# Sigmoid attention and a gated feed-forward on one core: weight decoding in two tiles over all stages, operands made ahead, token differences on VectorE

## Chip, core, metric

The kernel runs on one NeuronCore of a Trainium2 chip. The metric is the device time of one execution in microseconds (us), the median of several runs. TensorE (PE) multiplies, VectorE (DVE), ScalarE (ACT) and GpSimd (POOL) do elementwise work, and SyncE (SP) issues nearly all DMAs, in order.

## What is computed

```python
scores = scale * np.matmul(q, k.transpose(0, 1, 3, 2)) - np.log(S)   # q, k, v: (8, 12, 448, 64)
attn = 1.0 / (1.0 + np.exp(-scores))
attn_out = np.matmul(attn, v)
x = np.ascontiguousarray(attn_out.transpose(0, 2, 1, 3)).reshape(B * S, H * D)   # (3584, 768)
h = x @ w_in                                   # (768, 2048)
g = h * np.clip(h + 3.0, 0.0, 6.0) / 6.0
return (g @ w_out).astype(np.float32)          # (2048, 768)
```

The weights come as 64-bit floats and are turned into 32-bit floats on the chip.

## The kernel before

**Pairs and products.** Both matrix products use a scheme with 7 block products in place of 8: `P1, P5, P6, P2, P7, P3, P4`, in this order. Tokens are taken as pairs of batches, `n` = 0 to 3; the four blocks of `x` are the two batches (of 448 tokens) by the two halves of the features. Each of the seven left operands is a block or a sum of differences of blocks. Full precision comes from splitting each operand in a high and a low part (fp32r) and adding three passes; so an operand for product `k` and feature chunk `c` (0 to 2) is a tile `X[n, k, c]` with two halves, made by `put`: a cast (L216) and a subtraction (L217), both on DVE. `minus` (L221) makes the differences, on POOL. `t_ops` sets out seven puts and four differences for each chunk. The tiles of `X` have one buffer each, so pair `n` can fill one only when pair `n - 1` has used it for its last product.

**Stages.** TensorE's order is attention of batches 0 to 3, the first feed-forward product of pair 0, attention of batch 4, product of pair 1, batches 5 and 6, product of pair 2, batch 7, product of pair 3, and then the second product of all pairs. A batch has 21 steps: for each, `scores` fills two PSUM banks (L169, L174), `sigmoid` on ACT (L180) reads them, and `av` (L194, L200) multiplies by v, two steps behind. When the 128 columns of two heads are complete, `take` copies one bank (ACT, L208) and adds the other (DVE, L209) into `xr[b, hp]`; only then may the two banks be filled again, three steps later.

**Quads.** The product of a pair is eight `quad`s, of 7 x 9 matmuls each (L279). Several products share a bank: P6, P7 and P4 are added to the bank of P1. So `seed2` (DVE, L295), which reads that bank after P6, has to be done before P7 starts, and `h22` (DVE, L299), which reads it after P7, before P4. The gates (ACT L313, DVE L316), differences of gates (L320 to L326) and the splitting of weights for the next quad (`split_w1`: ACT L252, DVE L253) fill ACT and DVE beside. The last gate of a stage reads the bank of P1, which attention's scores then use again.

**Weight decoding.** `prep(which, j, place, gap)` decodes block `j` of eight of the first (`which` = 0) or second weight matrix, in two halves `u`. `load` fetches raw 64-bit words to `st` (two buffers), `head` (ACT, L100) and `body` (five operations on DVE, L106 to L112, and an addition on POOL, L115) make 32-bit floats of a half in the tile `wt`, `sums` (POOL, L122, four operations) makes the weight sums of the scheme, and `store` writes all seven to DRAM, from where the quads load them again (L246). `wt` has a single buffer.

**Order.** Every piece is given a place in planned us with `at(place, f, *args)`. The list is sorted by place, and on PE, ACT, DVE and POOL the instructions run in that order, each engine in order by itself; a late instruction holds those behind it. SP's order is chosen by the framework's scheduler. Planned time `TU` = 1.863 us stands for one block product.

```python
    for j in range(HF):
        prep(0, j, 12 + 15.2 * j, 6)
    for j, place in enumerate([marks[0] + 10 + 30 * i for i in range(3)] + [marks[1] + 10 + 30 * i for i in range(3)] + [starts[2] + 5, starts[2] + 25]):
        prep(1, j, place, 8)
```

`starts[n]` is the planned start of a stretch of attention, `marks[n]` its end, where the quads of pair `n` start. So the first matrix is decoded beside batches 0 to 3, the second beside the quads of pairs 0 and 1 (three blocks each) and batches 5 and 6 (two).

Of the kernel before, what the change touches and what calls it, by code (L numbers as in the profile page):

```python
# [43 lines left out]
def tile_kernel(ctx: ExitStack, tc: tile.TileContext, qk, vP, w8, outT):  # L44
# [37 lines left out]
    def prep(which, j, place, gap):  # L82

        src = w8[which]
        st, wt = {}, {}
        slots = ((P1, P2), (P4, NW))

        def two(u):
            a, b = slots[u]
            return wt[0][:, a : b + 1 : b - a]  # L90

        def load(u):
            st[u] = att.tile([P, 2, W, 2], I32, tag="st", name=f"st_{which}_{j}_{u}", bufs=2)
            s = src[j, :, 2 * u * W : 2 * (u + 1) * W].rearrange("p (h n) t -> p h n t", h=2)
            nc.sync.dma_start(out=st[u], in_=s)

        def head(u):
            if u == 0:
# [1 line left out]
            nc.scalar.activation(two(u), st[u][:, :, :, 1].bitcast(F32), AF.Abs, bias=0.0, scale=2.0**-112)  # L100

        def body(u):
            low, high = st[u][:, :, :, 0], st[u][:, :, :, 1]
            a, e = two(u), high.bitcast(F32)
            ai = a.bitcast(I32)
            nc.vector.tensor_scalar_min(a, a, F64_TOP)  # L106
            nc.vector.tensor_scalar(out=ai, in0=ai, scalar1=3, scalar2=None, op0=ALU.logical_shift_left)
            nc.vector.scalar_tensor_tensor(
                out=ai, in0=high, scalar=-(2**31), in1=ai, op0=ALU.bitwise_and, op1=ALU.bitwise_or
            )  # L110
            nc.vector.tensor_scalar(out=high, in0=ai, scalar1=-(2**23), scalar2=None, op0=ALU.bitwise_and)
            nc.vector.scalar_tensor_tensor(  # L112
                out=e, in0=low.bitcast(U32), scalar=2.0**-52, in1=e, op0=ALU.mult, op1=ALU.mult
            )
            nc.gpsimd.tensor_tensor(out=a, in0=a, in1=e, op=ALU.add)  # L115

        def sums():
            w = wt[0]
            for o, x, y, op in (
                (P5, NW, P4, ALU.add), (P6, P5, P1, ALU.subtract), (P7, P1, NW, ALU.subtract), (P3, P2, P6, ALU.subtract)  # L120
            ):
                nc.gpsimd.tensor_tensor(out=w[:, o], in0=w[:, x], in1=w[:, y], op=op)  # L122

        def store():
            w = wt[0]
            if which == 0:
                nc.sync.dma_start(out=wd1[j], in_=w[:, :NW])
# [90 lines left out]
        X[n, k, c] = x  # L218

    def minus(o, x, y):  # L220
        nc.gpsimd.tensor_tensor(out=xr[o], in0=xr[x], in1=xr[y], op=ALU.subtract)  # L221
# [235 lines left out]
    for n, bs in enumerate(runs):
        steps = [(b, m, r) for b in bs for m in range(HC) for r in range(LC)]  # L460
# [90 lines left out]
```

## Time and profile before

| | us |
|---|---|
| median of 3 runs (lowest, highest) | 1287.93 (1285.09, 1294.91) |
| the profiled execution | 1288.0 |
| its span, first to last instruction | 1286.2 |
| PE busy | 1143.3 (89%) |
| DVE busy | 839.1 (65%) |
| ACT busy | 613.5 (48%) |
| POOL busy | 203.5 (16%) |
| mean granted TensorE clock | 0.942 |

The profile shows one execution. In its rows, `L174 PE MATMUL sc<-qk` is line 174 of the kernel, the engine, the operation and what it writes and reads; in a timeline, the first number is the start in the span, the second the duration, and the brackets give how long the engine sat idle before it, and what ended that. A row of the waits is "engine line <- what it waited for: us in total, times, longest". A row of the stretches gives for each engine the busy time and, in brackets, the number of instructions, and at its end the granted clock (1.00 is full speed), the share of the DMA engines and GB/s. `za` is the bank shared by P1, P6, P7 and P4, `zb` the others.

### The profile page before, as it was taken

To read this page: it belongs to the slowest core of one execution; us is meant where nothing else is said; L and a number is where in the kernel's file an instruction comes from. 1 tells how busy PE (TensorE), PEld (TensorE's weight loads), DVE (VectorE), ACT (ScalarE), POOL (GpSimd) and SP (SyncE) were. 2 spreads that over 40 slices of the span, in tenths; PEclk is the share of its full clock that TensorE was granted. 3 is DMA by queue.
4 is the path that set the end of the run, shared out by engine and by line. 5 is a ranking of instruction groups with operands and counts; after the bars stand their busy time and mean duration, and the time that the engine had idled before them with its cause. 6 is when DMAs were issued, how large, how long until landed. Compare 5 with 4: busy or idle time off the path is not lost.

```text
span 1286.2 us, 17828 instructions
## 1 busy us (share of the span) xinstructions
PE 1143.3 (89%) x6720; PEld 884.8 (69%) x6720; DVE 839.1 (65%) x1096; ACT 613.5 (48%) x830; POOL 203.5 (16%) x150
## 2 busy tenths in 40 slices
PE   8676777888799886978999987999999999999998
PEld 3222223777747776633899557989999999999997
DVE  3388534877798877596667594776565565565563
ACT  5443455433265433655444643445445544545542
POOL 2245343312240322053000130000000000000000
PEclk9777788988899988989999988999999999999999
DMA  6744456767646876554677339757645344345341
GB/s 241 264 165 158 175 191 211 273 242 258 228 131 190 269 261 223 186 170 144 209 236 229 132 116 336 217 189 282 247 158 186 144 157 158 117 166 204 115 137 64
DMA packets 90661, 250.20 MB, mean 195 GB/s; under 512 B 10064, under 2 KB 62672, under 8 KB 85072
## 3 DMA queue, kind: packets, MB, share of 16 engines
q1 hardware_dynamic: 90432, 249.01, 56.4%
q8 instruction: 52, 0.85, 0.3%
q14 instruction: 33, 0.27, 0.1%
q10 hardware_dynamic: 144, 0.07, 0.0%
HBM read 164.63 MB, written 84.41 MB: 194 GB/s over the span
## 4 chain that ended last, share of the span: by engine, by line
PE 48%; DVE 5%; DMA 2%; issue 1%; POOL 1%; ACT 1%; ACTq 0%; DVEq 0%; POOLq 0%
PE y L404 21%; PE yb L404 11%; PE za L279 8%; PE zb L279 6%; DVE x L217 2%; DMA raw<-wd 1%; DVE x L216 1%; PE sc L174 1%; PE pv L200 1%; DVE w L253 1%; DVE xr L209 0%; POOL wt L122 0%; DMA wd<-wt 0%; POOL xr L221 0%; ACT w L252 0%
## 5 line engine op out<-in xcount | busy, mean ns | idle before, releaser
L279 PE MATMUL za<-x,w 128*128 128x448 f32 x1152 | 273.4, 388 | 60.1 <-DVE zb L295 47.6
L404 PE MATMUL y<-x,w 128*128 128x448 f32 x1344 | 308.8, 365 | 0.0
L279 PEld LDWEIGHTS za<-x,w 128*128 128x128 f32 x1152 | 227.0, 200 | 94.1 <-DVE zb L295 53.2
L404 PEld LDWEIGHTS y<-x,w 128*128 128x128 f32 x1344 | 252.4, 188 | 20.0
L253 DVE TENSOR_TENSOR w<-w,w 128x768 fp32r<-128x768 f32 x112 | 107.3, 958 | 152.2 <-ACT w L252 150.8
L180 ACT ACTIVATE a<-sc,bias_s 128x896 f32<-128x896 f32 x168 | 168.2, 1009 | 77.4 <-PE sc L174 58.7
L174 PE MATMUL sc<-qk 64*64 64x448 f32 x1152 | 164.0, 589 | 44.7 <-ACT a L180 39.6
L279 PE MATMUL zb<-x,w 128*128 128x448 f32 x864 | 196.3, 372 | 2.7 <-DVE x L216 1.7
L252 ACT CAST w<-w 128x768 fp32r<-128x768 f32 x112 | 93.6, 836 | 191.4 <-PE yb L404 183.8
L253 DVE TENSOR_TENSOR w<-raw,w 128x768 fp32r<-128x768 f32 (+1 forms) x128 | 125.6, 982 | 90.0 <-ACT w L252 82.5
L279 PEld LDWEIGHTS zb<-x,w 128*128 128x128 f32 x864 | 166.8, 193 | 17.9 <-DVE x L216 2.1
L404 PE MATMUL yb<-x,w 128*128 128x448 f32 x672 | 172.6, 365 | 0.0
L200 PE MATMUL pv<-a,v 64*64 64x448 f32 x1152 | 165.6, 580 | 6.9 <-DVE xr L209 6.9
L174 PEld LDWEIGHTS sc<-qk 64*64 64x64 f32 x1152 | 51.9, 144 | 121.6 <-issue 59.3
L404 PEld LDWEIGHTS yb<-x,w 128*128 128x128 f32 x672 | 126.2, 188 | 10.0
L387 DVE TENSOR_TENSOR x<-gr,x 128x896 fp32r<-128x896 f32 x112 | 121.4, 1084 | 5.6 <-ACT x L386 5.6
L115 POOL TENSOR_TENSOR wt<-wt,st 128x768 f32<-128x768 f32 x32 | 62.5, 1954 | 366.8 <-DVE st L112 347.3
L200 PEld LDWEIGHTS pv<-a,v 64*64 64x64 f32 x1152 | 55.3, 144 | 81.8 <-issue 67.4
L386 ACT CAST x<-gr 128x896 fp32r<-128x896 f32 x112 | 105.3, 940 | 5.6 <-DMA gr<-gd 5.6
L252 ACT CAST w<-raw 128x768 fp32r<-128x768 f32 (+1 forms) x128 | 95.5, 748 | 13.5 <-DMA raw<-wd 13.5
L221 POOL TENSOR_TENSOR xr<-xr,xr 128x448 f32<-128x448 f32 x48 | 63.1, 1319 | 188.7 <-DVE x L217 186.5
L217 DVE TENSOR_TENSOR x<-xr,x 128x448 fp32r<-128x448 f32 x84 | 87.3, 1039 | 2.9
(48 smaller groups left out, 794.6 us busy)
## 6 DMA issues: line engine op xcount, KB each, us to landing
gr<-gd SPq DMA_DIRECT2D x28, 1792.0 KB, 8.0
raw<-wd SPq DMA_DIRECT2D x96, 384.0 KB, 3.6
gd<-ga SPq DMA_DIRECT2D x96, 224.0 KB, 3.5
qk<-qk SPq DMA_DIRECT2D x47, 448.0 KB, 5.1
gd<-gc SPq DMA_DIRECT2D x64, 224.0 KB, 2.8
st<-wi SPq DMA_DIRECT2D x16, 768.0 KB, 4.3
st<-wo SPq DMA_DIRECT2D x16, 768.0 KB, 5.8
v<-vP SPq DMA_DIRECT2D x48, 224.0 KB, 4.4
```

The costliest lines, as they stand in the source:

```text
L115: nc.gpsimd.tensor_tensor(out=a, in0=a, in1=e, op=ALU.add)
L174: nc.tensor.matmul(sc[halves[h], j, :S], k[halves[j], ks], q[halves[j]], start=True, stop=True)
L180: nc.scalar.activation(a, sc[:, :, :S], AF.Sigmoid, bias=bias_s, scale=scale)
L200: nc.tensor.matmul(pv[b, hp][h][halves[j], :S], v[halves[h], j * NC + c], a[halves[h], j], start=c == 0 and not (second and shared), stop= ...
L217: nc.vector.tensor_tensor(out=x[:, 1], in0=xr[q], in1=x[:, 0].bitcast(F32), op=ALU.subtract)
L221: nc.gpsimd.tensor_tensor(out=xr[o], in0=xr[x], in1=xr[y], op=ALU.subtract)
L252: nc.scalar.copy(h, src)
L253: nc.vector.tensor_tensor(out=l, in0=src, in1=h.bitcast(F32), op=ALU.subtract)
L279: nc.tensor.matmul(z[k][:, :S], w[:, wu, c * P : (c + 1) * P], X[n, k, c][:, xu], start=i == 0 and k in (P1, P5), stop=i == 3 * HC - 1, sk ...
L386: nc.scalar.copy(x[:, 0], src)
L387: nc.vector.tensor_tensor(out=x[:, 1], in0=src, in1=x[:, 0].bitcast(F32), op=ALU.subtract)
L404: nc.tensor.matmul(z[k][e][:, :S], w[:, wu, e * P : (e + 1) * P], x[:, xu], start=u == 0 and i == 0 and k in (P1, P5, P2, P3), stop=u == H ...
```

## The change

**Decoding.** `wt` becomes two tiles: `wa` (two buffers) holds the four decoded blocks, `ws` (one buffer) the four sums. The five DVE operations of a half, issued together before, get places 1.4 apart, the four sums places 1.3 apart. The stores of the first matrix are seven, as for the second, instead of one; for both they are called in two groups, the blocks (`wa`) first and the sums (`ws`) five planned us later. The raw loads are called 9 instead of 7 planned us ahead. The first matrix is decoded every 22.5 planned us instead of 15.2, halves 11.2 apart instead of 6, so that its last blocks fall beside the quads of pair 0. The second matrix is decoded every 46, halves 15 apart, from late in pair 0's quads to the attention of batch 7; four and a half of its blocks fall beside the quads of pairs 1 and 2 or at their edges.

**Operands.** `minus` moves from POOL to DVE. `t_ops` takes one chunk and three places: the operands P1 and P2 need only the first batch, and the first difference with P5 one block more of the second. For pair 1 to 3 these are placed behind the products P1, P5, P2 of the previous pair's last quad (or after the take, if that is later), so before or during the attention that makes the second batch; the rest follows the last take, or the end of the quads for pair 1. A pause of 9 planned us ahead of pair 3's quads is dropped.

```diff
-            nc.sync.dma_start(out=st[u], in_=s)
...
+            nc.sync.dma_start(out=st[u], in_=src[j, :, 2 * u * W : 2 * (u + 1) * W])
...
-                wt[0] = att.tile([P, NW + 1, W], F32, tag="wt", name=f"wt_{which}_{j}")
...
+                wt["a"] = att.tile([P, 4, W], F32, tag="wa", name=f"wa_{which}_{j}", bufs=2)
...
+        def sums(i):
+            if i == 0:
+                wt["s"] = att.tile([P, 4, W], F32, tag="ws", name=f"ws_{which}_{j}")
...
+        def store(w, ks):
+            for i, k in enumerate(ks):
+                d = wd1[j][:, k] if which == 0 else wd2[k][:, j]
+                nc.sync.dma_start(out=d, in_=wt[w][:, i])
 
         for u in range(2):
-            at(place + u * gap - 7, load, u)
+            at(place + u * gap - 9, load, u)
             at(place + u * gap, head, u)
-            at(place + u * gap + 0.9, body, u)
-        at(place + 2 * gap, sums)
-        at(place + 2 * gap + 5, store)
+            for i in range(6):
+                at(place + u * gap + 0.9 + 1.4 * i, body, u, i)
+        for i in range(4):
+            at(place + gap + 10.5 + 1.3 * i, sums, i)
+        at(place + gap + 12, store, "a", (P1, P2, P4))
+        at(place + gap + 17, store, "s", (P5, P6, P7, P3))
...
     def minus(o, x, y):
-        nc.gpsimd.tensor_tensor(out=xr[o], in0=xr[x], in1=xr[y], op=ALU.subtract)
+        nc.vector.tensor_tensor(out=xr[o], in0=xr[x], in1=xr[y], op=ALU.subtract)
+
+    def t_ops(n, c, ready, gap):
...
+        b11, b12, b21, b22 = ((2 * n, c), (2 * n + 1, c), (2 * n, c + HC), (2 * n + 1, c + HC))
+        first, upper, both = ready
+        at(first[0], put, n, P1, c, b11)
+        at(first[1], put, n, P2, c, b21)
+        at(upper, minus, b11, b12, b11)
+        at(upper + 0.01, put, n, P5, c, b11)
+        for i, part in enumerate((
+            (put, n, P3, c, b22), (minus, b12, b22, b12), (minus, b22, b22, b11), (put, n, P6, c, b22), (put, n, P7, c, b12),
+            (minus, b21, b21, b22), (put, n, P4, c, b21),
+        )):
+            at(both + gap * i, *part)
...
-        if n == len(runs) - 1:
-            now += 9.0
...
+                    taken[b, hp] = now + 1.4
...
+    for n in range(NT):
+        free = marks[n - 1] + HF * q if n else 0.0
+        for c in range(HC):
+            own = [taken[2 * n + (h % 2), c + HC * (h // 2)] for h in range(4)]
+            late = 0.4 * c
+            first = (max(free - 5.6 * TU + 1.1 * c, own[0] + late), max(free - 2.6 * TU + 1.1 * c, own[2] + late))
+            upper = max(free - 4.6 * TU + 1.7 * c + 0.5, own[1] + late, first[0] + 0.1)
+            if max(own) < free:
+                both = free - 0.5 + 7 * c
+                t_ops(n, c, (first, upper, both), 0.9)
+            else:
+                t_ops(n, c, (first, upper, max(own[3], first[1] + 0.1, upper + 0.1)), 1.0 if n < NT - 1 or c < 2 else 0.01)
     for j in range(HF):
-        prep(0, j, 12 + 15.2 * j, 6)
...
-        prep(1, j, place, 8)
...
+        prep(0, j, 11 + 22.5 * j, 11.2)
+        prep(1, j, marks[0] + 80 + 46 * j, 15)
```

TensorE's order is the same in both. Three places on other engines follow, before and now. In the names, the numbers after a tile are its indices and, last, a running number; lines of the changed kernel are up to 13 higher from `prep` on.

DVE at the program's start: the decode of the first half of block 0 (`wt_0_0` or `wa_0_0`), the first two takes (`xr_0_0`, `xr_0_3`). Before:

```order
L209 TENSOR_TENSOR xr_0_0_211<-pv_0_0_1_162,xr_0_0_211 128x448
L106 TENSOR_SCALAR wt_0_0_196<-wt_0_0_196 128x2x384
L107 TENSOR_SCALAR wt_0_0_196<-wt_0_0_196 128x2x384
L108 SCALAR_TENSOR_TENSOR wt_0_0_196<-st_0_0_0_139,wt_0_0_196 128x2x384
L111 TENSOR_SCALAR st_0_0_0_139<-wt_0_0_196 128x768
L112 SCALAR_TENSOR_TENSOR st_0_0_0_139<-st_0_0_0_139 128x768
L209 TENSOR_TENSOR xr_0_3_257<-pv_0_3_1_203,xr_0_3_257 128x448
```

And now, on the same engine at the same place, with the first operand (`x_0_0_0`) of pair 0:

```order
L104 TENSOR_SCALAR wa_0_0_189<-wa_0_0_189 128x768
L214 TENSOR_TENSOR xr_0_0_210<-pv_0_0_1_162,xr_0_0_210 128x448
L106 TENSOR_SCALAR wa_0_0_189<-wa_0_0_189 128x768
L221 CAST x_0_0_0_226<-xr_0_0_210 128x448
L222 TENSOR_TENSOR x_0_0_0_226<-xr_0_0_210,x_0_0_0_226 128x448
L108 SCALAR_TENSOR_TENSOR wa_0_0_189<-st_0_0_0_130,wa_0_0_189 128x768
L112 TENSOR_SCALAR st_0_0_0_130<-wa_0_0_189 128x768
L114 SCALAR_TENSOR_TENSOR st_0_0_0_130<-st_0_0_0_130 128x768
L214 TENSOR_TENSOR xr_0_3_259<-pv_0_3_1_202,xr_0_3_259 128x448
```

The block of five is taken apart, and operand P1 of pair 0, which stood behind both batches before, is made as soon as its first block is taken.

DVE in the last quad of pair 0, from the last differences of the quad before to `seed2` (`zb_0_7_5`). Before:

```order
L320 TENSOR_TENSOR ga_0_6_2394<-g12_0_6_2428,ga_0_6_2394 128x448
L321 TENSOR_TENSOR ga_0_6_2394<-gc_0_6_2415,ga_0_6_2394 128x448
L324 TENSOR_TENSOR gc_0_6_2415<-gc_0_6_2415,g12_0_6_2428 128x448
L326 TENSOR_TENSOR gt_0_6_2477<-g21_0_6_2452,ga_0_6_2394 128x448
L295 TENSOR_TENSOR zb_0_7_5_2508<-za_0_7_2442,sne_0_7_2490 128x448
```

And now, from the third of the four differences on:

```order
L329 TENSOR_TENSOR gc_0_6_2400<-gc_0_6_2400,g12_0_6_2413 128x448
L331 TENSOR_TENSOR gt_0_6_2458<-g21_0_6_2430,ga_0_6_2379 128x448
L221 CAST x_1_0_1_2461<-xr_2_1_1050 128x448
L222 TENSOR_TENSOR x_1_0_1_2461<-xr_2_1_1050,x_1_0_1_2461 128x448
L104 TENSOR_SCALAR wa_1_0_2319<-wa_1_0_2319 128x768
L221 CAST x_1_0_2_2483<-xr_2_2_1156 128x448
L222 TENSOR_TENSOR x_1_0_2_2483<-xr_2_2_1156,x_1_0_2_2483 128x448
L226 TENSOR_TENSOR xr_2_0_931<-xr_3_0_1271,xr_2_0_931 128x448
L221 CAST x_1_1_0_2487<-xr_2_0_931 128x448
L222 TENSOR_TENSOR x_1_1_0_2487<-xr_2_0_931,x_1_1_0_2487 128x448
L300 TENSOR_TENSOR zb_0_7_5_2501<-za_0_7_2420,sne_0_7_2475 128x448
```

Ahead of `seed2` now stand three operands P1 of pair 1 (the first just above this piece), a decode step, a difference and the first operand P5.

SP while batches 1 and 2 are computed: the stores of block 1 of the first matrix (`wd1_1`), raw loads (`st`), and loads of q, k and v. Before:

```order
L127 DMA wd1_1_58<-wt_0_1_356 128x2688
L151 DMA qk_1_4_487<-qk 128x896
L152 DMA v_1_4_488<-vP 128x448
L151 DMA qk_1_2_553<-qk 128x896
L95 DMA st_0_3_0_600<-wi 128x1536
```

And now, in the same queue:

```order
L132 DMA wd1_1_58<-wa_0_1_417 128x384 x2
L156 DMA qk_1_2_556<-qk 128x896
L157 DMA v_1_2_557<-vP 128x448
L156 DMA qk_1_5_605<-qk 128x896
L157 DMA v_1_5_606<-vP 128x448
L132 DMA wd1_1_58<-wa_0_1_417 128x384
L89 DMA st_0_2_1_702<-wi 128x1536
L132 DMA wd1_1_58<-ws_0_1_654 128x384 x4
L156 DMA qk_2_0_683<-qk 128x896
```

One store has become seven, and the load of batch 2's first q and k stands behind the four that wait for POOL's sums.

More of the change, by code (lines that the diff above doesn't have):

```diff
@@ L85, in prep @@
         st, wt = {}, {}
[L86 to L90, printed above, removed]
         def load(u):
-            st[u] = att.tile([P, 2, W, 2], I32, tag="st", name=f"st_{which}_{j}_{u}", bufs=2)
-            s = src[j, :, 2 * u * W : 2 * (u + 1) * W].rearrange("p (h n) t -> p h n t", h=2)
-            nc.sync.dma_start(out=st[u], in_=s)
+            st[u] = att.tile([P, 2 * W, 2], I32, tag="st", name=f"st_{which}_{j}_{u}", bufs=2)
@@ L102, in body @@
[L102 to L127, printed above, removed]
-            else:
-                for k in range(NW):
-                    nc.sync.dma_start(out=wd2[k][:, j], in_=w[:, k])
+                wt["a"] = att.tile([P, 4, W], F32, tag="wa", name=f"wa_{which}_{j}", bufs=2)
@@ new lines, in head, with body @@
+            a, _, _, _, e = parts(u)
+            nc.scalar.activation(a, e, AF.Abs, bias=0.0, scale=2.0**-112)
+        def body(u, i):
+            a, ai, low, high, e = parts(u)
+            if i == 0:
+                nc.vector.tensor_scalar_min(a, a, F64_TOP)
+            elif i == 1:
+                nc.vector.tensor_scalar(out=ai, in0=ai, scalar1=3, scalar2=None, op0=ALU.logical_shift_left)
+            elif i == 2:
+                nc.vector.scalar_tensor_tensor(
+                    out=ai, in0=high, scalar=-(2**31), in1=ai, op0=ALU.bitwise_and, op1=ALU.bitwise_or
+                )
+            elif i == 3:
+                nc.vector.tensor_scalar(out=high, in0=ai, scalar1=-(2**23), scalar2=None, op0=ALU.bitwise_and)
+            elif i == 4:
+                nc.vector.scalar_tensor_tensor(
+                    out=e, in0=low, scalar=2.0**-52, in1=e, op0=ALU.mult, op1=ALU.mult
+                )
+            else:
+                nc.gpsimd.tensor_tensor(out=a, in0=a, in1=e, op=ALU.add)
@@ new lines, in sums @@
+        def sums(i):
+            if i == 0:
+                wt["s"] = att.tile([P, 4, W], F32, tag="ws", name=f"ws_{which}_{j}")
+            (a11, a12, a22, a21), (s1, s2, s3, s4) = ([w[:, k] for k in range(4)] for w in (wt["a"], wt["s"]))
+            o, x, y, op = (
+                (s1, a21, a22, ALU.add), (s2, s1, a11, ALU.subtract), (s3, a11, a21, ALU.subtract), (s4, a12, s2, ALU.subtract)
+            )[i]
+            nc.gpsimd.tensor_tensor(out=o, in0=x, in1=y, op=op)
+        def store(w, ks):
+            for i, k in enumerate(ks):
+                d = wd1[j][:, k] if which == 0 else wd2[k][:, j]
+                nc.sync.dma_start(out=d, in_=wt[w][:, i])
@@ L457, in tile_kernel @@
     runs = [(0, 1, 2, 3), (4,), (5, 6), (7,)]
-    marks, starts = [], []
+    marks, starts, taken = [], [], {}
+    q = NW * TU
     for n, bs in enumerate(runs):
```

29 lines of the change are left out of this document (7 added, 22 removed).

## Prediction

> **What bounds the kernel now.** I first cut the profiled execution where TensorE changes from attention to products and back; the borders are the first matmul of each kind. The view gives busy time, granted clock and DMA share per stretch:
>
> ```profile
> core 0: us, PE busy (x) PEld busy (x) DVE busy (x) ACT busy (x) POOL busy (x), PEclk, DMA share, GB/s
> 0.00:215.50 215.50, 155.04 (x1344) 55.69 (x1344) 117.88 (x148) 109.09 (x128) 78.92 (x65) 0.83 0.57 200
> 215.50:356.60 141.10, 114.56 (x512) 101.50 (x508) 103.16 (x138) 51.84 (x83) 31.46 (x20) 0.90 0.72 245
> 356.60:393.10 36.50, 33.43 (x338) 14.11 (x337) 35.50 (x53) 25.84 (x30) 15.64 (x12) 1.00 0.40 127
> 393.10:528.60 135.50, 113.78 (x511) 101.09 (x508) 101.83 (x137) 51.52 (x83) 29.17 (x18) 0.90 0.72 239
> 528.60:613.30 84.70, 72.72 (x674) 29.90 (x673) 63.44 (x81) 52.07 (x61) 32.82 (x24) 0.94 0.50 162
> 613.30:716.50 103.20, 103.20 (x510) 94.02 (x508) 66.91 (x106) 46.56 (x77) 0.00 (x0) 1.00 0.70 223
> 716.50:749.00 32.50, 32.03 (x338) 12.70 (x337) 21.83 (x33) 24.60 (x28) 10.25 (x8) 1.00 0.25 79
> 749.00:873.30 124.30, 109.82 (x505) 97.39 (x506) 84.87 (x131) 51.64 (x84) 5.29 (x5) 0.95 0.65 225
> 873.30:1286.00 412.70, 408.72 (x2017) 378.41 (x2015) 243.71 (x275) 200.31 (x258) 0.00 (x0) 1.00 0.46 165
> ```
>
> In this order the rows are A0 (four batches), Q0, A1 (one batch), Q1, A2 (two), Q2, A3 (one), Q3 and Y. Q2, A3 and Y show TensorE without a gap at full clock, and POOL decodes nothing there: they are the floors, 103.2 for eight quads, 32.5 for a batch, 412.7. With 4 x 32.5 + 3.8 (the first load) for A0 and 65 for A2 the floor is 1088.5 us. What lies above it, 198 us, is A0 82, Q0 38, A1 4, Q1 32, A2 20, Q3 21.
>
> The waits of A0 alone, then one of them followed through four engines' timelines:
>
> ```profile
> ACT wt L100 <- DMA wd<-wt: 52.3, 6, 13.0
> ```
> ```profile
> PE sc L174 <- ACT a L180: 35.0, 5, 9.2
> PE sc L169 <- ACT a L180: 13.7, 2, 7.0
> ```
> ```profile
> 27.32 3.99 POOL L122 TENSOR_TENSOR wt<-wt 128x384 f32<-128x384 f32 x4
> ```
> ```profile
> 31.34 0.33 SPq L127 DMA_DIRECT2D wd<-wt  x1
> ```
> ```profile
> 36.11 0.89 ACT L100 ACTIVATE wt<-st 128x768 f32<-128x768 f32 x1 [7.77 <-DMA wd<-wt]
> ```
> ```profile
> 37.95 1.77 PE L169 MATMUL sc<-qk 64*64 64x448 f32 x8 [6.99 <-ACT a L180]
> ```
>
> The single tile `wt` is still being stored when ACT wants to write the next block's first half. ACT's sigmoids stand behind that instruction, and TensorE behind them: 48.7 us idle.
>
> In Q0 the wait is another one. Its total, and the longest case on DVE, POOL and PE:
>
> ```profile
> PE za L279 <- DVE zb L295: 24.9, 7, 6.8
> ```
> ```profile
> 322.91 0.55 DVE L106 TENSOR_SCALAR wt<-wt 128x768 f32<-128x768 f32 x1
> ```
> ```profile
> 326.56 0.61 DVE L316 SCALAR_TENSOR_TENSOR g<-g,za 128x448 f32<-128x448 f32 x1
> 327.09 1.98 DVE L320 TENSOR_TENSOR ga<-g,ga 128x448 f32<-128x448 f32 x1
> 329.11 1.31 DVE L321 TENSOR_TENSOR ga<-gc,ga 128x448 f32<-128x448 f32 x1
> 330.34 1.41 DVE L324 TENSOR_TENSOR gc<-gc,g 128x448 f32<-128x448 f32 x1
> 331.67 1.41 DVE L326 TENSOR_TENSOR gt<-g,ga 128x448 f32<-128x448 f32 x1
> 333.00 1.74 DVE L253 TENSOR_TENSOR w<-raw,w 128x768 fp32r<-128x768 f32 x1
> 334.67 0.62 DVE L295 TENSOR_TENSOR zb<-za,sne 128x448 f32<-128x448 f32 x1
> ```
> ```profile
> 326.72 1.87 POOL L115 TENSOR_TENSOR wt<-wt,st 128x768 f32<-128x768 f32 x1 [11.37 <-DVE st L112]
> 328.67 5.26 POOL L122 TENSOR_TENSOR wt<-wt 128x384 f32<-128x384 f32 x4
> ```
> ```profile
> 335.35 1.86 PE L279 MATMUL za<-x,w 128*128 128x448 f32 x4 [6.78 <-DVE zb L295]
> ```
> Half a decode holds DVE from 322.91 to 326.56, 3.65 us in one block. Then four operations with two SBUF operands take 1.36, 0.69, 0.8 and 0.8 longer than alone (0.62, as that shape takes at 383.46 below), and for the split behind them (L253) I take another 0.8: POOL's 7.1 us cost DVE 4.4, 60%. `seed2` (L295) comes late, and product P7, which overwrites the bank it reads, has only P2's 1.8 us of cover.
>
> A stall also costs clock. Two gaps and the 1.9 us behind each:
>
> ```profile
> 413.70:416.10 2.40, 0.04 (x2) 0.01 (x1) 2.40 (x5) 1.35 (x2) 0.00 (x0) 0.96 1.06 395
> 416.10:418.00 1.90, 1.90 (x5) 1.73 (x6) 1.83 (x3) 0.00 (x0) 0.00 (x0) 0.50 1.13 378
> ```
> ```profile
> 242.50:244.10 1.60, 0.04 (x1) 0.04 (x1) 1.60 (x4) 1.35 (x2) 0.00 (x0) 1.00 1.07 399
> 244.10:246.00 1.90, 1.90 (x9) 1.76 (x10) 1.83 (x3) 0.00 (x0) 0.00 (x0) 1.00 1.04 344
> ```
>
> After 2.4 us the clock was halved, after 1.6 it was not. Q0 holds 26.5 us of idle PE in its 38 above the floor, so I add about half of each stall for clock.
>
> **The change, part by part.** The prices of an operand (`put`, from one start to the next) with POOL at rest, and of a difference on POOL:
>
> ```profile
> 383.04 0.38 DVE L216 CAST x<-xr 128x448 fp32r<-128x448 f32 x1
> 383.46 0.62 DVE L217 TENSOR_TENSOR x<-xr,x 128x448 fp32r<-128x448 f32 x1
> 384.00 0.62 DVE L209 TENSOR_TENSOR xr<-pv,xr 128x448 f32<-128x448 f32 x1
> ```
> ```profile
> L221 POOL TENSOR_TENSOR xr<-xr,xr 128x448 f32<-128x448 f32 x48 | 63.1, 1319 | 188.7 <-DVE x L217 186.5 <-DVE x L216 0.9
> ```
>
> A put is 0.96. The 48 differences leave POOL (63.1 us) for DVE. None stands there before: between 0.62 alone and 1.98 beside POOL (the same shape at 383.46 and 327.09); I take 0.54, the step from 383.46 to 384.00, and charge the lock apart.
>
> *A0.* With two `wa` tiles a head waits only for the store of the tile before last, 22.5 planned us back; that store lands 5 us after its sums. The 48.7 us and their clock go. What is late next is DVE in the pair's second batch: 15 puts x 0.96 + 12 differences and 6 takes x 0.54 + 2.9 half decodes x 3.65 = 34.7, and POOL's 9 us per 22.5 cost 60% of 12.9 = 7.7: 42.4 in 32.5. The pv banks give three steps of 1.5 (32.5/21) less copy and add (twice the add's 0.62), 3.3. Stall 6.6, clock 3.4: **A0 144**. ACT's heads keep their 0.89 beside sigmoids that wait anyway; uncovered, 16 x 0.89 = 14 us, not in the sum.
>
> *Quads with a decode.* The five DVE operations now stand 1.4 apart. Alone a quad takes DVE 66.9/8 = 8.4 of 12.9 us; with a half decode and 60% of (1.9 + 2.6) of POOL it is 14.7. The first four quads of Q0 hold one half each. In the second, from the first's `h22` to P7's start, TensorE takes 10.9 us; DVE's queue holds three gates, four differences, `seed2` and `h22` itself (9 x 0.54), three splits (2.2, from the 1.74 less its lock), a half decode (3.65), and 60% of 6.9 us of POOL: 14.9, so `seed2` is some 3.9 late. The others, with fewer of POOL's sums, come to 2.6, 2.4 and 2.2 by the same addition: 11, with clock 18. One half in quad 6: 4.
>
> *Last quads.* They now also make operands: in Q0 nine puts and three differences, 10.3, beside 3.65 of decode and 1.1 of lock: 23.4 in 12.9. Counted from the quad's start in the order shown with the change: a gate and four differences of the quad before, three puts, a decode step, a difference and a put end at 8.6, then `seed2` at 9.2, where P7 wants it at 7.3: 2 late. Ten operations more (7.6) bring `h22` to 17.4, where P4 wants it at 12.9: 4.5 late. 10 with clock; the rest runs into A1. **Q0 103 + 32 = 135.** In Q1 and Q2 only six puts are there (19 in 12.9): 2 late. Q1 has 2.5 decodes, apart from each other: 9.4 idle in all, 15 with clock, **118**. Q2, clean before, gets 2.5 as well: 12 idle, 18 with clock, **121**; here the change costs.
>
> *A1, A2, A3.* The last gate stands behind these operations on DVE and frees a score bank 2 us late; takes lag less than the 3.3 except beside POOL's sums. I put 4.5, 4.5 and 3.5 above the floors: **37, 69.5, 36**. If the lock's 60% were all of POOL's time, 4 more each.
>
> *Q3.* All operands but the third column's are ready. After the last take (0.9 behind A3) DVE is 3.8 late and needs 4.2 more for P6's operand; TensorE wants it at 4.9: 4.0, then `seed2` 1.6, 8 with clock. One wait stays:
>
> ```profile
> 788.18 0.83 ACT L252 CAST w<-raw 128x768 fp32r<-128x768 f32 x1 [7.19 <-DMA raw<-wd]
> ```
>
> That weight load stands behind Y's large loads in SP's queue, which follow the weights of Q3's first quad; those are taken earlier now, so I leave 5 of the former 10, clock included (between 0 and 10). **Q3 117**, with 1 for the rest. Y unchanged.
>
> *SP.* Forty-eight more stores at about 0.33, 16 us of issue on a queue that mostly waits. Between nothing and the 12 us lead of the loads behind them; I take nothing, and give the other end to a rival.
>
> Sum: 144 + 135 + 37 + 118 + 69.5 + 121 + 36 + 117 + 412.7 = 1190. The profiled execution took 1288.0 for a span of 1286.2, and the median is 1287.9, so 1.8 comes on top: **1192 us**.
>
> **The rivals.** *Short stalls cost no clock.* Where the new gaps stay under a threshold, the clock goes that I charged to them, some 25 of the 35 us in my sum: 1167. Against it speaks the 2.40 us gap above. In the Trainium skill, "TensorE: Matmul & The Clock Gate", section "Why this matters for your kernels", it is gaps of more than about 3 us that bring the half clock; nearly all my stalls would be free by it, but the trace disagrees: 2.40 us brought 0.50.
>
> *The spread works fully.* If DVE's queue absorbs the spaced decodes, the quads keep 5 us each instead of 15 to 32, A0 ends at 136, the others at 34, 67, 34 and Q3 at 112: 1118. For it: 4.5 us of free DVE per quad. Against: the two tight places per quad.
>
> *The gain is given back.* DVE stays late as in Q0 now: Q0 and Q1 141 and 135 as before, Q2 135 like them, A0 160, the A stages 43, 75, 38, Q3 124: 1266. For it: demand above the span in Q0's first and last quads. Against: the halves in Q1 and Q2 stand apart.
>
> *SP holds the loads: slower.* Each block's last four stores wait in order for POOL's sums, and the next q, k loads stand behind. What such a load takes to land, and SP's waits for sums today (in all, times, longest):
>
> ```profile
> qk<-qk SPq DMA_DIRECT2D x47, 448.0 KB, 5.1
> ```
> ```profile
> SPq L127 <- POOL wt L122: 37.7, 8, 7.8
> ```
>
> If the stores come to the head of the queue more than 7 us before the sums (12 lead less 5.1), TensorE waits in each of 16 decodes; at 7.8 each that is 125 and half for clock: 1192 + 187 = 1379. For it: DVE's lag delays the sums; against: the same lag delays TensorE.
>
> *It doesn't free ACT.* The heads wait for raw weights instead, whose loads stand behind stores; then A0 keeps 82 in place of 10: 1264. Against: they are called 9 planned us ahead.
>
> **How the numbers follow.** My forecast (1150 to 1235) 0.55, short stalls free 0.12, full spread 0.11, given back 0.14, SP 0.04, ACT not freed 0.04. The range 1135 to 1250 leaves out most of the full spread and the upper part of the cases around 1265, about 0.2 together with SP. Some 0.03 of those cases pass 1275. A change within 1% could not be told from none here; faster by more 0.93, the same 0.03, slower 0.04.
>
> **What would show it.** A0: no ACT wait on the store of decoded weights; TensorE waiting for the take's add instead, some 7 us, between 40 and 75 us. Q0: `seed2` waits of 2 to 4 us in the first four quads and in the last, none between. Q2: PE busy under its span for the first time, POOL busy some 22 us. A put's second half: near its 0.62, except beside a decode's sums. I am wrong if PE's waits in the quads sum to under 15 or over 55 us, or if SP's q, k loads appear among PE's waits.

## The result and the profile after

| | before | after |
|---|---|---|
| median (lowest to highest) | 1291.35 (1285.09 to 1294.91) | 1176.78 (1169.5 to 1182.7) |
| the profiled execution, its span | 1288.0, 1286.2 | 1182.7, 1180.9 |
| DVE busy | 839.1 | 826.9 |
| POOL busy | 203.5 | 144.9 |
| mean granted clock | 0.942 | 0.977 |

The times are in us. The ratio is 0.9115, with a 95% interval of 0.9048 to 0.9182. The measured median lies inside the forecast range of 1135 to 1250; the predicted 1192 us is 15 us above the median, and 9 above the profiled execution.

The view of the stretches, cut as for the prediction (A0, Q0, A1, Q1, A2, Q2, A3, Q3, Y):

```profile
core 0: us, PE busy (x) PEld busy (x) DVE busy (x) ACT busy (x) POOL busy (x), PEclk, DMA share, GB/s
0.00:143.65 143.65, 134.01 (x1344) 69.90 (x1344) 98.87 (x134) 105.53 (x124) 44.02 (x37) 0.99 0.75 253
143.65:272.79 129.14, 113.88 (x508) 101.03 (x505) 111.80 (x161) 52.18 (x84) 31.87 (x20) 0.92 0.77 259
272.79:310.23 37.44, 33.88 (x338) 13.07 (x337) 31.19 (x53) 26.40 (x31) 5.77 (x5) 0.95 0.61 191
310.23:427.02 116.79, 108.61 (x509) 96.36 (x505) 93.22 (x142) 50.72 (x82) 19.80 (x13) 0.97 0.77 256
427.02:491.44 64.42, 63.53 (x674) 25.48 (x673) 45.04 (x73) 50.56 (x59) 14.66 (x11) 1.00 0.65 222
491.44:610.81 119.37, 108.87 (x508) 97.31 (x505) 94.41 (x141) 50.45 (x82) 21.38 (x13) 0.96 0.72 240
610.81:644.68 33.87, 32.19 (x337) 14.90 (x336) 27.93 (x42) 26.30 (x31) 7.35 (x6) 1.00 0.41 135
644.68:759.94 115.26, 109.11 (x508) 97.12 (x505) 80.50 (x130) 50.06 (x82) 0.00 (x0) 0.96 0.70 240
759.94:1180.90 420.96, 416.80 (x2017) 378.25 (x2015) 243.98 (x275) 200.02 (x258) 0.00 (x0) 1.00 0.46 162
```

A0 lost 72 us, Q0 12, Q1 19, A2 20, Q3 9, and Q2, clean before, gained 16. The largest of TensorE's waits:

```profile
PE za L284 <- DVE zb L300: 30.4, 17, 3.4
PE za L284 <- DVE snh L304: 6.5, 6, 2.5
PE pv L205 <- DVE xr L214: 5.1, 2, 4.2
PE sc L179 <- DVE g L321: 5.0, 3, 2.4
PE sc L179 <- DMA qk<-qk: 3.8, 1, 3.8
```

No wait of TensorE on ACT behind a store is left; `seed2` (now L300) and `h22` (L304) lead, and a last gate (L321) holds the first scores of A1, A2 and A3 for 2.4, 0.9 and 1.7. One of the waits for `seed2` in Q2, with DVE, POOL and PE beside each other:

```profile
521.12 1.71 DVE L258 TENSOR_TENSOR w<-raw,w 128x384 fp32r<-128x384 f32 x1
522.76 0.61 DVE L321 SCALAR_TENSOR_TENSOR g<-g,za 128x448 f32<-128x448 f32 x1
523.29 0.91 DVE L325 TENSOR_TENSOR ga<-g,ga 128x448 f32<-128x448 f32 x1
524.23 1.33 DVE L326 TENSOR_TENSOR ga<-gc,ga 128x448 f32<-128x448 f32 x1
525.48 1.43 DVE L329 TENSOR_TENSOR gc<-gc,g 128x448 f32<-128x448 f32 x1
526.84 1.42 DVE L331 TENSOR_TENSOR gt<-g,ga 128x448 f32<-128x448 f32 x1
528.17 0.95 DVE L258 TENSOR_TENSOR w<-raw,w 128x768 fp32r<-128x768 f32 x1
529.04 0.62 DVE L300 TENSOR_TENSOR zb<-za,sne 128x448 f32<-128x448 f32 x1
```
```profile
519.89 2.52 POOL L118 TENSOR_TENSOR wa<-wa,st 128x768 f32<-128x768 f32 x1 [13.83 <-DVE st L114]
522.49 1.22 POOL L127 TENSOR_TENSOR ws<-wa 128x384 f32<-128x384 f32 x1
...
526.39 1.38 POOL L127 TENSOR_TENSOR ws<-wa,ws 128x384 f32<-128x384 f32 x1
```
```profile
529.72 1.49 PE L284 MATMUL za<-x,w 128*128 128x448 f32 x3 [3.43 <-DVE zb L300]
```

While POOL adds and sums (two more sums stand between the two shown), four differences of gates take 0.91 to 1.43 instead of 0.62, and the split at 521.12 takes 1.71 instead of 0.55; the gate at 522.76, whose second operand lies in PSUM, takes its 0.61. POOL's 7.9 us cost DVE 3.8 here, and TensorE waits 3.43.

Y took 421.0 where 412.7 was forecast, because each of its matmuls took 368 ns there instead of 365 at the same granted clock of 1.00. Of the experiments below, three took 421.0 as well (differences on GpSimd, no sums, old places) and the others 412.9; therefore they are compared by the time at which Y begins as well (before 873.3, after 759.9). The four executions of the kernel before lie at 1285 to 1288 and at 1295, a similar distance apart; that Y makes this difference too is likely, not shown.

### The profile page after: what moved, and what is told of

The parts are those of the page before. It is cut to its first block, busy times and chain, and to the rows that moved or that the text cites. A ratio compares the mean times of both kernels' runs of the same rounds, so it can differ in the third digit from the quotient of the medians.

```text
span 1180.9 us, 17909 instructions
## 1 busy us (share of the span) xinstructions
PE 1120.9 (95%) x6720; PEld 893.4 (76%) x6720; DVE 826.9 (70%) x1144; ACT 612.2 (52%) x830; POOL 144.9 (12%) x102
## 4 chain that ended last, share of the span: by engine, by line
PE 70%; DVE 11%; DMA 8%; issue 6%; POOL 2%; ACT 1%; SPq 0%; ACTq 0%; DVEq 0%; POOLq 0%
PE y L409 24%; PE za L284 12%; PE yb L409 12%; PE zb L284 8%; PE sc L179 6%; PE pv L205 6%; DMA raw<-wd 3%; DVE w L258 2%; DMA v<-vP 2%; PE sc L174 1%; ACT w L257 1%; DVE g L321 1%; DMA st<-wo 1%; PE pv L199 1%; POOL ws L127 1%
## 5 line engine op out<-in xcount | busy, mean ns | idle before, releaser
L409 PE MATMUL y<-x,w 128*128 128x448 f32 x1344 | 313.9, 368 | 0.0
L284 PE MATMUL za<-x,w 128*128 128x448 f32 x1152 | 270.0, 385 | 38.1 <-DVE zb L300 30.4
L284 PEld LDWEIGHTS za<-x,w 128*128 128x128 f32 x1152 | 223.3, 197 | 72.9 <-DVE zb L300 37.7
L409 PE MATMUL yb<-x,w 128*128 128x448 f32 x672 | 175.0, 368 | 0.0
L179 PE MATMUL sc<-qk 64*64 64x448 f32 x1152 | 151.8, 547 | 9.9 <-DVE g L321 5.0
L205 PE MATMUL pv<-a,v 64*64 64x448 f32 x1152 | 152.5, 546 | 5.1 <-DVE xr L214 5.1
L392 DVE TENSOR_TENSOR x<-gr,x 128x896 fp32r<-128x896 f32 x112 | 121.4, 1084 | 4.8 <-ACT x L391 4.8
L118 POOL TENSOR_TENSOR wa<-wa,st 128x768 f32<-128x768 f32 x32 | 64.3, 2008 | 485.9 <-DVE st L114 471.9
L179 PEld LDWEIGHTS sc<-qk 64*64 64x64 f32 x1152 | 54.6, 135 | 69.7 <-issue 45.5
L318 ACT ACTIVATE gc<-snh,bias 128x448 f32<-128x448 f32 x32 | 21.4, 670 | 110.9 <-DVE snh L304 96.4
L222 DVE TENSOR_TENSOR x<-xr,x 128x448 fp32r<-128x448 f32 x84 | 65.1, 775 | 2.9
```

Of the source, the lines that this page charges most:

```text
L179: nc.tensor.matmul(sc[halves[h], j, :S], k[halves[j], ks], q[halves[j]], start=True, stop=True)
L205: nc.tensor.matmul(pv[b, hp][h][halves[j], :S], v[halves[h], j * NC + c], a[halves[h], j], start=c == 0 and not (second and shared), stop= ...
L222: nc.vector.tensor_tensor(out=x[:, 1], in0=xr[q], in1=x[:, 0].bitcast(F32), op=ALU.subtract)
L284: nc.tensor.matmul(z[k][:, :S], w[:, wu, c * P : (c + 1) * P], X[n, k, c][:, xu], start=i == 0 and k in (P1, P5), stop=i == 3 * HC - 1, sk ...
L318: nc.scalar.activation(g[o], src(o), AF.Relu, bias=bias_3, scale=1.0)
L392: nc.vector.tensor_tensor(out=x[:, 1], in0=src, in1=x[:, 0].bitcast(F32), op=ALU.subtract)
```

## The experiments

The ratios are to the kernel before, measured beside each. Times of stages and waits are those of the one profiled execution of each kernel, and a row of waits covers the whole execution. "Head" of the waits is the ACT instruction that starts a half of a decode.

**One tile.**

```diff
-                wt["a"] = att.tile([P, 4, W], F32, tag="wa", name=f"wa_{which}_{j}", bufs=2)
+                wt["a"] = att.tile([P, 4, W], F32, tag="wa", name=f"wa_{which}_{j}", bufs=1)
```

> The changed kernel with one buffer for the tile of decoded blocks instead of two, all else as changed. Theory of the prediction (A0's gain is ScalarE freed from the store of the single tile): a head comes 22.5 planned us after the one before, the first group of stores is issued 23.2 after that one and takes some 4 to land, the sums that read the tile end near 26.6, so each head waits 5 to 8 us; A0 143.7 goes to 175 to 195 with the clock, a wait of ScalarE's head on the store of decoded blocks is back with 25 to 45 us, total 1215 to 1245. Rival (the wider spacing of 22.5 for 15.2 did it, the second tile is not needed): A0 within 5 of 143.7, total under 1190.

Measured: 1186.3, ratio 0.9205 (0.9166 to 0.9245); Y begins at 770.1. The rows are A0, the head's wait, one such head with the sum before it, and the score that waits behind:

```profile
0.00:153.51 153.51, 134.96 (x1345) 51.81 (x1345) 95.73 (x134) 105.30 (x124) 42.87 (x37) 0.96 0.71 236
```
```profile
ACT wa L99 <- POOL ws L127: 26.9, 6, 7.7
```
```profile
36.58 1.00 POOL L127 TENSOR_TENSOR ws<-wa,ws 128x384 f32<-128x384 f32 x1
```
```profile
37.61 0.89 ACT L99 ACTIVATE wa<-st 128x768 f32<-128x768 f32 x1 [3.81 <-POOL ws L127]
```
```profile
39.45 1.77 PE L179 MATMUL sc<-qk 64*64 64x448 f32 x8 [3.03 <-ACT a L185]
```

A0 rises by 10 us, not by 30 to 50: my theory missed and the rival came nearer. What holds the tile is now the last sum, 26.9 planned us after its head (11.2 + 10.5 + 4 x 1.3), against a period of 22.5: 4.4 late, and 4.5 was measured on average (26.9/6). The single waits run from 1.1 to 7.7, so part of this agreement is luck. The stores of the blocks are not what ends the wait: in A0 they landed 1.5 to 3.2 us before the last sum was done, and the sums now lie in a tile of their own.

**Two tiles alone**, in the kernel before: its places, its block of five and its differences, with the new tiles and stores.

```diff
-                wt[0] = att.tile([P, NW + 1, W], F32, tag="wt", name=f"wt_{which}_{j}")
+                wt["a"] = att.tile([P, 4, W], F32, tag="wa", name=f"wa_{which}_{j}", bufs=2)
...
+                wt["s"] = att.tile([P, 4, W], F32, tag="ws", name=f"ws_{which}_{j}")
```

> The kernel before with only the changed tiles (two of four decoded blocks, one of four sums, stores in two groups); places, spacing, order of the decode operations, differences on GpSimd and operands as before. Theory of the prediction: the wait of the head (52.3 us) goes; the decode now asks DVE for 16 x 3.65 us and POOL for all its work inside A0, so A0 falls from 215.5 only to 160 to 175, Q0 to Y as before, total 1235 to 1250. Rival (spacing did it; DVE and POOL are overfull in A0 with all eight decodes there): A0 stays above 200, total above 1270.

Measured: 1237.1, ratio 0.9595 (0.9548 to 0.9642).

```profile
0.00:170.63 170.63, 144.40 (x1344) 75.60 (x1345) 124.36 (x148) 108.42 (x128) 82.01 (x66) 0.94 0.77 254
```
```profile
PE pv L205 <- DVE xr L214: 21.9, 7, 5.9
```

As expected: ACT is free (0.6 us of its heads' wait on stores is left), and what is late next is DVE, the takes' adds (in A0 10.7 of the 21.9, and 8.3 more behind L199). The two tiles and the division of the stores were not tried apart.

**The places alone**, in the kernel before.

```diff
-        prep(0, j, 12 + 15.2 * j, 6)
-    for j, place in enumerate([marks[0] + 10 + 30 * i for i in range(3)] + [marks[1] + 10 + 30 * i for i in range(3)] + [starts[2] + 5, starts[2] + 25]):
-        prep(1, j, place, 8)
+        prep(0, j, 12 + 22.5 * j, 6)
+        prep(1, j, marks[0] + 80 + 46 * j, 8)
```

> The kernel before with only the changed places of the decodes (first matrix from 12 every 22.5 with its halves 6 apart as before, second matrix from 80 behind Q0's start every 46, halves 8 apart); tile, block of five operations, differences and operands as before. Theory after the first four runs (the single tile is held some 22 us, from the head to the landing of its stores, so a period of 15.2 must stall ScalarE and one of 22.5 need not): the head's wait on the store falls from 52.3 to under 15, A0 from 215.5 to 150 to 165; Q0 and Q2 now hold halves as blocks of 3.65 (Q0 140 to 150, Q2 118 to 128), A2 70 to 76; total 1205 to 1235. Rival (the period is not the cause, the tile or the store groups are): A0 above 195, total above 1250.

Measured: 1237.2, ratio 0.9602 (0.9557 to 0.9647). A0 and the head's wait:

```profile
0.00:156.61 156.61, 136.84 (x1344) 73.67 (x1344) 94.37 (x124) 105.88 (x124) 56.98 (x49) 0.96 0.67 232
```
```profile
ACT wt L100 <- DMA wd<-wt: 5.4, 4, 3.3
```

The head's wait falls from 52.3 to 2.1 in A0 (from 62.2 to 5.4 in the whole execution) and A0 by 59 with the old single tile. The total came out 2 above the range; Q1 (127.8) and Q3 (124.7), for which the expectation has no figure, are 11 and 9 above the changed kernel's.

**The old places** in the changed kernel.

```diff
-        prep(0, j, 11 + 22.5 * j, 11.2)
-        prep(1, j, marks[0] + 80 + 46 * j, 15)
+        prep(0, j, 12 + 15.2 * j, 6)
+    for j, place in enumerate([marks[0] + 10 + 30 * i for i in range(3)] + [marks[1] + 10 + 30 * i for i in range(3)] + [starts[2] + 5, starts[2] + 25]):
+        prep(1, j, place, 8)
```

> The changed kernel with the decodes back at the places of before (first matrix every 15.2 from 12 with halves 6 apart, all in A0; second matrix three in Q0, three in Q1, two in A2, halves 8 apart); two tiles, spaced operations, differences on DVE and early operands as changed. Theory (the places carry about half of the gain, since two tiles alone gave 1237): A0 from 143.7 back to 160 to 172, A2 from 64.4 to 72 to 80, Q2 from 119.4 to 105 to 112, Q0 and Q1 within 6 of the changed kernel's; total 1195 to 1220. Rival (with two tiles and spaced operations the places don't matter): total within 8 of the changed kernel's.

Measured: 1187.4, ratio 0.9191 (0.9124 to 0.9258); Y begins at 763.7, 4 us after the changed kernel's. A0 and Q2:

```profile
0.00:156.79 156.79, 136.81 (x1344) 54.46 (x1345) 125.20 (x160) 108.25 (x128) 66.03 (x50) 0.97 0.82 275
514.83:619.19 104.36, 103.58 (x508) 93.95 (x505) 72.17 (x118) 46.58 (x77) 0.00 (x0) 1.00 0.69 220
```

A0 costs 13 more (16 to 28 were expected), A2 9 and Q1 6, but Q2 gives back 15, and A1, A3 and Q3 9: with the rest of the change in place, where the decodes lie moves the loss more than it removes it. In A0 the heads now wait 15.4 us for raw words and 4.1 for stores. By its total the run stands between theory and rival; by Y's begin it is within the rival's 8 us, so the theory missed.

**Differences on GpSimd** in the changed kernel.

```diff
-        nc.vector.tensor_tensor(out=xr[o], in0=xr[x], in1=xr[y], op=ALU.subtract)
+        nc.gpsimd.tensor_tensor(out=xr[o], in0=xr[x], in1=xr[y], op=ALU.subtract)
```

> The changed kernel with the 48 token differences back on GpSimd. Theory of the prediction: DVE gets back 48 x 0.54 = 26 us, GpSimd is busy 63 us more, of which 60% blocks DVE, 38; differences stand behind sums in GpSimd's queue where operands wait for them. Net a small loss: 5 to 20 us, total 1185 to 1200, most of it in A0 and in Q0's last quad. Rival (the move of the differences carries much of the gain): loss of 40 or more. Other rival (the move costs, DVE being the tight engine): gain of 5 to 15.

Measured: 1180.5, ratio 0.9162 (0.9114 to 0.9211); span 1180.9 and Y at 759.9, like the changed kernel. A0 147.6 (+3.9) and the other attentions (+4.2) pay, Q0 (125.3), Q1 (113.8) and Q2 (117.8) gain as much. No net difference that can be told, where a loss of 5 to 20 was expected. POOL is busy 62 us longer, and DVE, with 48 operations less, as long as before (826.2 for 826.9).

**Differences on DVE alone**, the opposite edit in the kernel before.

> The kernel before with only the 48 differences moved to DVE. Theory of the prediction: GpSimd's queue gets shorter in A0 (24 differences of 1.3), so sums and the store that frees the tile come a little earlier: A0 5 to 15 less, A2 2 to 6 less, Q stages as before: total 1265 to 1282. Rival (the differences on GpSimd and their port conflict were a main cost): total under 1250.

Measured: 1266.8, ratio 0.9845 (0.9794 to 0.9896), a small gain; A0 205.6 (-10), A1 and A2 together 6 less, as expected. TensorE's waits on the sigmoids in A0 fall from 48.7 to 40.8. The edit gains where the tile is held, and nothing that can be told once that is cured.

**The block of five** in the changed kernel.

```diff
-                at(place + u * gap + 0.9 + 1.4 * i, body, u, i)
+                at(place + u * gap + 0.9, body, u, i)
```

> The changed kernel with the five DVE operations of a half in one block again, all else as changed. Theory of the prediction (a block of 3.65 us ahead of seed2 is what makes it late): the waits of TensorE in the quads go from 36 to 50 to 65 us, with clock 15 to 25 us more, total 1195 to 1205. Rival (DVE's sum per quad decides, not the order inside it): waits and total within 5 us of the changed kernel's.

Measured: 1205.1, ratio 0.9355 (0.9305 to 0.9405); Y begins at 788.0.

```profile
PE za L284 <- DVE zb L300: 58.2, 18, 9.7
```

The waits for `seed2` go from 30.4 to 58.2 with the same DVE instructions (busy 840.8 instead of 826.9). The rival, that only DVE's sum counts and waits and total stay within 5 us, falls. With `h22` the waits are 63 us, inside the expected 50 to 65. Of the parts undone singly (second tile, places, differences, block, early operands) this costs most, 28 us.

**No operands in the last quads.**

```diff
-            first = (max(free - 5.6 * TU + 1.1 * c, own[0] + late), max(free - 2.6 * TU + 1.1 * c, own[2] + late))
-            upper = max(free - 4.6 * TU + 1.7 * c + 0.5, own[1] + late, first[0] + 0.1)
+            first = (max(free + 1.1 * c, own[0] + late), max(free + 1.1 * c, own[2] + late))
+            upper = max(free + 1.7 * c + 0.5, own[1] + late, first[0] + 0.1)
```

> The changed kernel without the operands made ahead in a stage's last quad: those of P1, P2 and P5 come when the quad is over. Theory of the prediction (the last quads pay for them: Q0 10, Q1 and Q2 some 3 each): Q0 falls by 5 to 10, Q1 and Q2 by 2 to 4, A1 and A3 rise by 3 to 6 and Q3's start by 2 to 5: total 1172 to 1182. Rival (they are a gain: without them the products after A1 to A3 start late): total 1190 or more, with waits of TensorE on operands of 8 us or more.

In this order some differences read an operand that has been replaced already; their number and kind are unchanged. Measured: 1172.7, ratio 0.9106 (0.9057 to 0.9155); Y begins at 756.2. Q0 and A1:

```profile
143.26:263.66 120.40, 110.57 (x507) 98.92 (x504) 101.71 (x142) 52.21 (x84) 31.45 (x19) 0.94 0.83 280
263.66:307.13 43.47, 36.69 (x337) 16.72 (x337) 40.75 (x72) 26.43 (x31) 6.32 (x6) 0.88 0.51 160
```

Q0 falls by 8.7, Q1 by 5.1, Q2 by 6.4; A1 rises by 6.0, A2 by 9.1, A3 by 2.8. The operands made ahead cost the quads about what they spare the attentions.

**No sums on POOL.**

```diff
-        for i in range(4):
-            at(place + gap + 10.5 + 1.3 * i, sums, i)
...
-        at(place + gap + 17, store, "s", (P5, P6, P7, P3))
+        at(place + gap + 17, store, "a", (P5, P6, P7, P3))
```

> The changed kernel without the four sums of each decode on GpSimd; the second group of stores writes decoded blocks in their place, so loads, stores and all DVE work stay. Theory of the prediction (60% of GpSimd's 4 to 5 us of sums blocks DVE, 2.6 us per decode, and the quads have no room): waits in the quads fall from 36 to 15 to 22 us, Q0 by 8 to 12, Q1 and Q2 by 4 to 7 each, A0 by 2 to 5; total 1150 to 1165. Rival (the sums lie in gaps of DVE and cost nothing): total within 5 us of the changed kernel's.

Measured: 1142.1, ratio 0.8862 (0.8825 to 0.8899). Y begins at 723.9, 36 before the changed kernel's, and the sum of the stretches and the largest wait read:

```profile
sum 1144.90, PE 1099.68 PEld 876.17 DVE 797.99 ACT 612.12 POOL 64.25; mean PE 122.19 PEld 97.35 DVE 88.67 ACT 68.01 POOL 7.14
```
```profile
PE za L282 <- DVE zb L298: 20.4, 15, 3.0
```

DVE executes the same instructions in 29 us less (826.9 before): POOL's 81 us of sums had blocked it for that long, 36%, and that was worth 36 us up to Y. The total went beyond my range, but the waits did not: those for `seed2` and `h22` fell from 36.9 to 28.2 and not to 15 to 22. A0 gave 7.4, and the granted clock was higher, 0.991 to 0.995 in the four executions where those of the changed kernel had 0.977 to 0.986.

**Splits behind `seed2` and `h22`.** DVE's half of the next quad's first two weight splits is placed 0.95 and 0.85 of a product later.

```diff
+        return lambda: nc.vector.tensor_tensor(out=l, in0=src, in1=h.bitcast(F32), op=ALU.subtract)
...
             at(place + (u - 7) * TU, split_w1, n, j, i)
+            at(place + (u - 7) * TU + (0.95, 0.85, 0.0, 0.0)[i] * TU, low_w1, n, j, i)
```

> The changed kernel with DVE's half of the first two weight splits of each quad moved behind seed2 and behind h22 (0.95 and 0.85 of a product later); ScalarE's casts and all else stay. Theory (what DVE does just ahead of seed2 and h22 is what TensorE waits for; a split is 0.96, up to 1.75 beside GpSimd): the 37 us of waits for seed2 and h22 fall to 15 to 25 and their clock with them, total 1150 to 1168. Rival (DVE's sum per quad decides: then the splits come late and P1, P6 wait for them): total within 6 of the changed kernel's and waits of TensorE on the splits of 8 us or more.

Measured: 1157.9, ratio 0.8972 (0.8926 to 0.9017); Y begins at 740.0.

```profile
PE za L289 <- DVE zb L305: 23.4, 16, 3.1
PE za L289 <- DVE snh L309: 5.4, 3, 4.1
```

The total came as expected, the mechanism in part: the waits fell from 37 to 29, where 15 to 25 were put down. DVE is busy 834.1 (826.9 before), so no work was saved, and the splits themselves appear in no wait of TensorE. In the two profiled executions most of the 20 us up to Y lies in the clock (mean 0.988 instead of 0.977); but the four executions of the changed kernel had 0.977, 0.984, 0.984 and 0.986 and the four of this one 0.982 to 0.988, so how much of that the edit gave stays open.

**Sums on DVE**, on top of that.

```diff
-            nc.gpsimd.tensor_tensor(out=o, in0=x, in1=y, op=op)
+            nc.vector.tensor_tensor(out=o, in0=x, in1=y, op=op)
```

> The kernel of the run before (weight splits behind seed2 and h22) with the 64 sums of the decodes on DVE at the same places instead of on GpSimd. Theory (a sum on GpSimd already takes DVE about 0.45 through the blocking, from DVE's 29 us less in the run without sums, and a 128x384 operation on DVE takes 0.55): nearly a wash, DVE busy within 10 of the run before, total 1150 to 1168. Rival (it is not the share but the moment: sums on GpSimd stretch whatever DVE does just then, seed2's chain too, while on DVE they stand where they were put): total 1130 to 1148. Other rival (DVE is the bound and blocking hid beside idle DVE): 1170 or more.

Measured: 1139.0, ratio 0.8815 (0.8769 to 0.8861), the fastest version; Y begins at 724.2.

```profile
sum 1137.10, PE 1089.40 PEld 871.97 DVE 833.24 ACT 612.80 POOL 63.45; mean PE 121.04 PEld 96.89 DVE 92.58 ACT 68.09 POOL 7.05
```
```profile
PE za L289 <- DVE zb L305: 22.5, 16, 3.3
```
```profile
L127 DVE TENSOR_TENSOR ws<-wa 128x384 f32<-128x384 f32 x32 | 17.6, 550 | 3.4 <-POOL wa L118 3.4
```

The theory was right on the work and wrong on the time: DVE gets 64 more instructions of 0.55, 35 us, and is busy 833.2 instead of 834.1. The rival's total came; its path through `seed2` did not, for those waits hardly changed (22.5 for 23.4). The gain lies in A0 (-6.5), A1 (-4.8) and Q0 (-4.0): TensorE's waits for the takes' adds fell from 5.9 to 2.1, and the clock rose (0.994 to 0.997 in the four executions, 0.982 to 0.988 without). On POOL a sum stretches what DVE is doing just then, on DVE it stands in the slot that it was given; that this moment is what was saved fits, but no run shows it apart.

**Decodes spread otherwise**, on the kernel with the splits moved.

```diff
-        prep(0, j, 11 + 22.5 * j, 11.2)
-        prep(1, j, marks[0] + 80 + 46 * j, 15)
+        prep(0, j, 11 + 18 * j, 9)
+        prep(1, j, marks[0] + 36 + 51.5 * j, 25.7)
```

> The kernel with the weight splits behind seed2 and h22, and the decodes spread more evenly: first matrix every 18 from 11 with halves 9 apart (ends near A0's end), second matrix from 36 behind Q0's planned start every 51.5 with halves 25.7 apart. Theory (each half taken out of Q0 saves some 3 there and finds room on DVE in A0, idle there for 47 of 144 us): Q0 from 122.6 to 112 to 118, A0 from 144.2 to 146 to 152, Q1, Q2 within 4; total 1145 to 1156. Rival (A0 is as full as the quads, by GpSimd's blocking and the period that approaches the tile's hold): A0 155 or more, total 1158 or more.

Measured: 1165.9, ratio 0.9024 (0.8973 to 0.9074); Y begins at 746.6, 6.6 later than without. Q0 fell by 3.8 and A0 did not rise (144.5), which speaks for the theory; but Q2 rose from 112.1 to 121.4, so the total missed. Its worst wait, in Q2's last quad, on PE and on DVE:

```profile
591.32 3.73 PE L289 MATMUL za<-x,w 128*128 128x448 f32 x9 [7.59 <-DVE zb L305]
```
```profile
588.59 2.13 DVE L222 TENSOR_TENSOR x<-xr,x 128x448 fp32r<-128x448 f32 x1
```

Half a decode and POOL's add had moved into a last quad, beside its operands. Q0's last quad shows the same (8.1).

## Why the prediction was right, and where it was not

*By stage* (forecast, measured): A0 144, 143.7; Q0 135, 129.1; A1 37, 37.4; Q1 118, 116.8; A2 69.5, 64.4; Q2 121, 119.4; A3 36, 33.9; Q3 117, 115.3; Y 412.7, 421.0. Up to Y it is 777 against 760. A2 and A3 were mis-sized by 7: I had charged a gate 2 us late and a lag of the takes. The gate cost 0.9 and 1.7 there (2.4 in A1), and the lag nothing. In Q0 I had put 2.2 to 3.9 in each of the first four quads and 4, clock included, in the sixth; the first waited 0.2, the second to fifth 2.5, 3.0, 0.8 and 2.6, the sixth not at all and the seventh 0.6. The last waited 2.9 and 2.6 for 2 and 4.5. The size held, then, and the places were one quad off. The quads' waits sum to 40, inside the 15 to 55. Y's 8 us were not foreseen; they hide half of the 17 us by which the stages before it were forecast too long, so that the 9 us to the profiled execution are partly luck. Two sums of the prediction are a little off and carry nothing: by their own terms the floor is 1089.3 and the full spread some 1122.

*A0: the number held, the reason only in part.* I gave the whole gain to the second tile. Either it or the longer period frees ACT (0.9595 and 0.9602 alone), and inside the changed kernel undoing one of them costs 4 to 10 us up to Y, with intervals of the ratio that overlap the changed kernel's own. That the takes' adds come next held: 5.9 us of waits for 7 forecast, though the longest, 4.2, stood at 91 us and not before 75.

*The quads.* That spacing the five operations matters was right and is the largest single term, 28 us. That DVE pays for POOL's time was right, but 60% was too much as a mean: over all sums 36%, in the wait shown above 3.8 of 7.9. The charge of 0.54 for each difference on DVE was real work and no time; on POOL they cost as much.

*Clock.* Two gaps of TensorE and what follows each, the first in Q1 of the profile after, the second in Q2 of the kernel with the splits moved:

```profile
331.50:333.40 1.90, 0.02 (x1) 0.00 (x0) 1.90 (x4) 1.35 (x2) 0.00 (x0) 1.00 1.04 394
333.40:335.30 1.90, 1.89 (x6) 1.74 (x7) 1.34 (x2) 0.00 (x0) 0.00 (x0) 0.65 1.07 397
334.10:337.50 3.40, 3.40 (x10) 3.01 (x10) 1.27 (x3) 0.14 (x1) 0.00 (x0) 0.52 1.04 370
337.50:339.40 1.90, 1.90 (x11) 1.73 (x10) 0.62 (x1) 0.99 (x2) 0.00 (x0) 1.00 0.93 346
```
```profile
515.20:517.60 2.40, 0.06 (x1) 0.00 (x0) 2.40 (x4) 1.35 (x2) 1.36 (x2) 1.00 0.52 190
517.60:519.50 1.90, 1.86 (x9) 1.74 (x10) 1.38 (x2) 0.00 (x0) 0.00 (x0) 1.00 0.89 315
```

After 1.9 us the clock was halved for 3.4 us, which loses 1.7; after 2.4 us in the other kernel it stayed at 1.00 (where, at 179.9, 1.8 us were followed by 0.61). In the profile after, the clock record has 13 such pieces before Y begins, ten of 3.41 us and three of 6.83: some 27 us lost beside 56 us of idle TensorE, so the half that I had added to each stall holds as a mean. For a single stall it doesn't: the length of the gap alone does not decide whether a piece of half clock follows. The rival of free short stalls (1167) is out because of the 27 us, though the median is nearer to its number (10 us) than to mine (15). The Trainium skill, "TensorE: Matmul & The Clock Gate", section "Why this matters for your kernels", speaks of gaps above some 3 us; the rows after the gap of 1.9 disagree with it.

*The other rivals.* SP: the first load (3.8) is the only q, k load among TensorE's waits. ACT not freed, the gain given back: the A0 and Q rows exclude them. The full spread (1118) asked that DVE absorb the decodes; it did so only in A2 and in the quads without one.

## What to carry over

When several edits cure one stall, undo each in the new kernel as well as adding each to the old: two of these gain 4% alone and 1% or less at the margin. On an in-order engine count what stands directly ahead of the instruction that another engine waits for; moving a split of 0.96 us from before it to behind it, for two such instructions in each of 32 quads, made the median 19 us lower with no work saved, of which the waits in the profile explain 8. Where stalls are near 2 us, compare the granted clock over several executions before a gain is put down to an edit. Work on GpSimd beside a loaded VectorE isn't free: here 64 sums on GpSimd cost VectorE as much time as it needed to do them itself.
